# Spreading weight conversion over two rows: fewer steps in batch 0, loads on another queue, block transposes first

## The chip, the cores and the metric

The kernel runs on one core of one Trainium2 chip. The metric is the device time of one execution in microseconds; the kernel before took 1356.45 us (median of three runs, 1355.39 to 1359.32).

## The reference

An attention with a threshold is followed by an MLP mixer. Queries, keys and values are float32; the four MLP weights are float64, because the reference multiplies them by a float64 factor.

```python
# q, k, v: (8, 8, 576, 64) float32
scores = scale * np.matmul(q, k.transpose(0, 1, 3, 2))          # 576 x 576 a head
thresh = np.max(scores, axis=-1, keepdims=True) - tau
scores = np.where(scores >= thresh, scores, -1000000000.0)
attn = np.exp(scores - np.max(scores, axis=-1, keepdims=True))
attn = attn / (np.sum(attn, axis=-1, keepdims=True) + 1e-09)
x = np.matmul(attn, v)            # then (B,H,S,D) -> (B, S, H*D) = (8, 576, 512)
# weights in float64: w_tok1 (576,256), w_tok2 (256,576), w_ch1 (512,1536), w_ch2 (1536,512)
h = np.maximum(x.transpose(0, 2, 1) @ w_tok1, 0.0) @ w_tok2
u = x + h.transpose(0, 2, 1)
out = (u + np.maximum(u @ w_ch1, 0.0) @ w_ch2).astype(np.float32)
```

## The kernel before

The kernel walks through 144 units. A unit is 128 rows of queries for the two heads of a pair; 18 units make a "row", which is one batch (row 0 is batch 0, row 1 is batch 1, and so on). In each unit TensorE makes scores, VectorE takes their maximum, GpSimd turns it into a bias, ScalarE applies Prelu (which does the threshold) and the exponential with its sum, and GpSimd normalizes. Two units later e is transposed, on TensorE in row 0 and by VectorE's 32 x 32 block transposes and sixteen DMAs a group of three units in the other rows. Then come the product with the values and, between the units of the next rows, the MLP of the batch that is done, handed out in small steps by `fill`.

The weights arrive as 64-bit words, in 31 pieces of at most 128 x 512. Each piece is loaded into one of four raw buffers and turned into float32 with integer and float operations on three engines. That is the work which the change moves.

```python
NRAW = 4                                      # raw buffers; one buffer `high` for the upper words
# 31 pieces: 3 of w_tok1, 4 of w_tok2, 12 of w_ch1, 12 of w_ch2

def load_piece(i):
    ...
    nc.sync.dma_start(out=like(raw, dst), in_=src)

def on_scalar(i, part):
        ...
        if part == 0:
            nc.scalar.activation(out=lo.bitcast(I32), in_=lo, func=AF.Copy, scale=2.0**-29)     # L193
        else:
            nc.scalar.activation(out=h2, in_=hi.bitcast(F32), func=AF.Abs)                      # L195

def on_vector(i, part):
        ...
        if part == 0:      # L203: max and mult on h2
        elif part == 1:    # L205: shift left, h2 -> dst
        else:              # L209: sign from hi, or into dst

def on_gpsimd(i):          # L217: dst = dst + lo (int32)

def weight(n):                                # the next n steps; three steps are a piece
    nonlocal steps_done
    for k in range(steps_done, min(steps_done + n, 3 * len(pieces) + 1)):
        i, part = divmod(k, 3)
        if part == 0:
            on_gpsimd(i - 1)
            if i:
                load_piece(i - 1 + NRAW)
        else:
            on_scalar(i + 1, part - 1)
        on_vector(i, part)
        steps_done = k + 1

def weight_to(x):                             # steps up to number x
    weight(max(int(x) - steps_done, 0))

def need(i):                                  # what the MLP calls before it uses piece i
    weight(3 * i + 4 - steps_done)
```

The MLP's channel part, a block of 256 tokens at a time (`ch1` is L507 with its eviction L508, `ch2` is L528):

```python
def ch1(j):
    need(7 + j)
    ...                       # 4 products with wc1[:, j], then ReLU on ScalarE
def ch2(t, part):
    need(7 + NJ + 3 * part + 2)
    if part == 0:
        s["ps"] = ps_mm.tile([P, NCC, P], F32, tag="mm", ...)     # ps_mm has two buffers
    ...                       # 3 products with wc2[:, 3*part ...]
return [(0.0067 * n, lambda j=j: ch1(j)) for j in range(NJ)] + [
    (2.6 if part or b else 3.0, lambda t=t, part=part: ch2(t, part)) for t in range(nt) for part in range(4)
]
```

The loop over units, cut to what orders the instructions (UB is 18, LAG is 2):

```python
for u in range(len(units) + LAG + 4):
    ...
    if on:
        scores(u)                             # L304, L309, L310
    ...
    if 0 < u <= len(units):
        norm(u - 1)                           # L333, L334, L337
    if b_now:
        weight(2)
    else:
        weight_to(2.25 * (u - (1 if visit else 1.5)))
        ...
    if back:
        if not in_blocks(wb):                 # row 0: TensorE transposes, L355, PSUM copies L357
            for i in range(3):
                turn(w, i)
        ...
    if b_now:
        fill(0.4)                             # MLP steps
    if back and in_blocks(wb):
        turn_blocks(w)                        # L367 on VectorE; every third unit 16 DMAs, L376
    if b_now:
        weight(2)
    if on and (b_now or not visit):
        weigh(u)                              # L319 Prelu, L326 exponential, with fill(0.2) three times
    elif b_now:
        fill(0.6)
    if b_now:
        weight(2)
    ...
    else:
        weight_to(2.25 * (u - 1))
    ...                                       # loads of q, k and v, prep (L286), values (L411, L416)
```

Of the kernel before, what the change touches and what calls it, by code (L numbers as in the profile page):

```python
# [9 lines left out]
F32 = mybir.dt.float32  # L10
# [7 lines left out]
P = 128  # L18
# [3 lines left out]
def kernel(  # L22
# [143 lines left out]

    raws = {}

    def load_piece(i):
        if i >= len(pieces):  # L170
            return
        dst, src = pieces[i]
        rows = dst.shape[0]
        n = 1
        for d in dst.shape[1:]:
            n *= d
        raw = raw_at[i % NRAW][0:rows, 0 : n * (2 if wide(i) else 1)].bitcast(src.dtype)
        nc.sync.dma_start(out=like(raw, dst), in_=src)
        if wide(i):
            words = raw.bitcast(U32).rearrange("p (n w) -> p n w", w=2)  # L180
            h2 = high[0:rows, 0:n]
            raws[i] = like(words[:, :, 0], dst), like(words[:, :, 1], dst), like(h2, dst)
        else:
            raws[i] = like(raw, dst)
# [35 lines left out]

    steps_done = 0

    def weight(n):

        nonlocal steps_done
        for k in range(steps_done, min(steps_done + n, 3 * len(pieces) + 1)):
            i, part = divmod(k, 3)
            if part == 0:  # L230
                on_gpsimd(i - 1)
                if i:
                    load_piece(i - 1 + NRAW)
            else:
                on_scalar(i + 1, part - 1)
            on_vector(i, part)
            steps_done = k + 1

    def weight_to(x):

        weight(max(int(x) - steps_done, 0))

    def need(i):

        weight(3 * i + 4 - steps_done)

    load_piece(0)
    load_v(0)
    for i in range(1, NRAW):
# [28 lines left out]
    def in_blocks(b):  # L278
        return b > 0
# [202 lines left out]
    def channel_mlp(b, uT, i):  # L482

        s = {}
        n = min(GR, 2 * S - GR * i)
        nt = n // P

        def turn_u():

            us, ut = s["us"], s["ut"]  # L490
            nc.vector.transpose(
                out=us[:, 0:nt].rearrange("q n a (c d) -> q c (n a) d", c=NCC),
                in_=uT[:, :, GR * i : GR * i + n].rearrange("q c (m r) -> q c m r", r=32),
            )

            def move(a, k):
                nc.sync.dma_start(out=ut[32 * a : 32 * a + 32, 0:nt, k, :], in_=us[32 * k : 32 * k + 32, 0:nt, a, :])

            moves.extend([lambda a=a, k=k: move(a, k) for a in range(4) for k in range(4)])

        def ch1(j):
            need(7 + j)
            if j == 0:
                s["g"] = work.tile([P, NJ, GR], F32, tag="g", bufs=1, name=f"g_{b}_{i}")
            ps = ps_mm.tile([P, GR], F32, tag="mm", name=f"c1_{b}_{i}_{j}")[:, 0:n]
            for c in range(NCC):
                nc.tensor.matmul(ps, lhsT=wc1[:, j, c, :], rhs=uT[:, c, GR * i : GR * i + n], start=(c == 0), stop=(c == NCC - 1))  # L507
            nc.scalar.activation(out=s["g"][:, j, 0:n], in_=ps, func=AF.Relu)  # L508
            if j == 1:
                s["us"] = work.tile([P, GR // P, 4, NCC * 32], F32, tag="us", bufs=1, name=f"us_{b}_{i}")  # L510
                if b:
                    s["ut"] = work.tile([P, GR // P, 4, NCC * 32], F32, tag="ut", bufs=1, name=f"ut_{b}_{i}")
                    turn_u()

        def ch2(t, part):
            need(7 + NJ + 3 * part + 2)
            t0 = GR * i + P * t
            if part == 0:
                s["ps"] = ps_mm.tile([P, NCC, P], F32, tag="mm", name=f"c2_{b}_{i}_{t}")
            ps = s["ps"]  # L520
            flat = ps.rearrange("q c d -> q (c d)")
            if part == 0 and not b:
                for c in range(NCC):
                    nc.tensor.matmul(
                        ps[:, c, :], lhsT=uT[:, c, t0 : t0 + P], rhs=ident, is_transpose=True, start=(c == 0), stop=False, skip_group_check=True
                    )
            for j in range(3 * part, 3 * part + 3):
                nc.tensor.matmul(  # L528
                    flat,
                    lhsT=s["g"][:, j, P * t : P * t + P],  # L530
                    rhs=wc2[:, j, :],
                    start=(j == 0 and b > 0),
                    stop=(j == NJ - 1),
                    skip_group_check=True,
                )
            if part == 3:
                o = s["us"][:, t].rearrange("q a x -> q (a x)")
                if b:
                    move_u()
                    nc.vector.tensor_add(  # L540
                        out=o.rearrange("q (c k d) -> q c k d", c=NCC, k=4),
                        in0=ps.rearrange("q c (k d) -> q c k d", k=4),
                        in1=s["ut"][:, t].rearrange("q k (c d) -> q c k d", c=NCC),
                    )
                else:
                    nc.vector.tensor_copy(out=o, in_=flat)
                nc.sync.dma_start(out=out[b : b + 2].rearrange("b s d -> (b s) d")[t0 : t0 + P, :], in_=o)

        return [(0.0067 * n, lambda j=j: ch1(j)) for j in range(NJ)] + [
            (2.6 if part or b else 3.0, lambda t=t, part=part: ch2(t, part)) for t in range(nt) for part in range(4)  # L550
        ]

    def move_u():
# [42 lines left out]

    prep(0)
    due = deque()
    b_now = 0
    LAG = 2  # L600

    def values_due(u):
# [11 lines left out]
    for u in range(len(units) + LAG + 4):  # L614
        on = u < len(units)
        if u == UB:
            late.close()
            ps_mm = ctx.enter_context(tc.tile_pool(name="ps_mm", bufs=2, space=bass.MemoryType.PSUM))
        if on:
            b_now, p0, t = units[u]  # L620
            n = b_now * NP + p0
        w = u - LAG
        back = 0 <= w < len(units)
        if on:
            scores(u)

        last = False
        visit = False
        if due and not in_blocks(due[0][1]):
            visit = due[0][0] <= u  # L630
            last = values_due(u)
        elif early:
            early.popleft()[1]()
        if 0 < u <= len(units):
            norm(u - 1)
        if b_now:
            weight(2)
        else:


            weight_to(2.25 * (u - (1 if visit else 1.5)))
            if visit and on:
                weigh(u)
        while copies:
            copies.popleft()()
        if last and u < UB:
            early.extend(token_mlp(0, range(NP // 2))[0])
        elif last:
            push(0)
        if back:  # L650
            wb, wp, wt = units[w]
            if not in_blocks(wb):
                for i in range(3):
                    turn(w, i)
            if wt % GU == GU - 1:
                g = wt // GU
                if g < 2:
                    split_middle(wb * NP + wp + g)
                due.append((u + (2 if in_blocks(wb) else 1), wb, wp, g))
        if b_now:  # L660
            fill(0.4)
        if back and in_blocks(wb):
            turn_blocks(w)
        if b_now:
            weight(2)
        if on and (b_now or not visit):
            weigh(u)
        elif b_now:
            fill(0.6)
        if b_now:  # L670
            weight(2)
        elif u == 0:
            on_scalar(0, 0)
            on_scalar(0, 1)
        else:
            weight_to(2.25 * (u - 1))
        if on:


            when = {3: (2, 0, 2), 4: (2, 2, 4), 5: (2, 4, 6), 6: (2, 6, 8), 8: (3, 0, 3), 0: (1, 3, 6), 1: (1, 6, 8)}  # L680
            if u == 0:
                load_qk(1, (nc.sync, nc.sync), range(0, 3))
            if t in when:
                m, lo, hi = when[t]
                if n + m < len(pairs):
                    load_qk(n + m, (nc.scalar if b_now else nc.sync,) * 2, range(lo, hi))
            if t in (3, 7) and n + 2 + t // 4 < len(pairs):
                load_v(n + 2 + t // 4)
            if t == 2:
                prep(n + 1)  # L690
            if t == 7 and n + 2 < len(pairs):
                prep(n + 2)
        if due and in_blocks(due[0][1]):
            values_due(u)

        if back and wt % GU == 0 or not on:
            move_u()
# [31 lines left out]
```

## Time and profile before

| what | us |
|---|---|
| time, median of three | 1356.45 |
| span of the profiled run | 1354.5 |
| TensorE matmul busy | 1308.3 |
| VectorE busy | 591.7 |
| ScalarE busy | 585.5 |
| GpSimd busy | 355.2 |
| conversion on VectorE (L203, L205, L209, all 31 pieces) | 63.0 |
| last conversion step begins (L217) | 188.3 |

The profile names engines PE (TensorE), DVE (VectorE), ACT (ScalarE), POOL (GpSimd) and SP (SyncE); a q behind the name is the engine's queue, where DMAs are issued. L numbers are lines of the kernel. A line of the timeline has the start, the length, the engine and line, what is written from what, and in brackets the idle time before it and who ended it. The row of conversion on VectorE is the sum of that engine's groups for those three lines (18.0, 19.0 + 3.8 and 17.5 + 4.7 us).

### The profile page before, as it was taken

To read this page: it belongs to the slowest core of one execution; us is meant where nothing else is said; L and a number is where in the kernel's file an instruction comes from. 1 tells how busy PE (TensorE), PEld (TensorE's weight loads), DVE (VectorE), ACT (ScalarE), POOL (GpSimd) and SP (SyncE) were. 2 spreads that over 40 slices of the span, in tenths; PEclk is the share of its full clock that TensorE was granted. 3 is DMA by queue.
4 is the path that set the end of the run, shared out by engine and by line. 5 is a ranking of instruction groups with operands and counts; after the bars stand their busy time and mean duration, and the time that the engine had idled before them with its cause. 6 is when DMAs were issued, how large, how long until landed. Compare 5 with 4: busy or idle time off the path is not lost.

```text
span 1354.5 us, 17794 instructions
## 1 busy us (share of the span) xinstructions
PE 1308.3 (97%) x6138; PEld 810.6 (60%) x6138; DVE 591.7 (44%) x1024; ACT 585.5 (43%) x1299; POOL 355.2 (26%) x683
## 2 busy tenths in 40 slices
PE   6888899999999999999999999999999999999998
PEld 4555656547574666565665567565656566575675
DVE  6878874435443444434344444435443454201000
ACT  6776654444444444443434444344333454120110
POOL 4565652222322222212122222222121222100000
PEclk9998999999999999999999999999999999999999
DMA  5434764545354444443445435534443453400000
GB/s 122 116 90 119 203 167 100 122 95 128 90 131 95 105 106 106 120 109 86 93 101 126 103 79 128 126 81 112 112 101 83 114 117 77 114 21 17 23 24 32
DMA packets 296539, 135.31 MB, mean 100 GB/s; under 512 B 204737, under 2 KB 289217, under 8 KB 296449
## 3 DMA queue, kind: packets, MB, share of 16 engines
q1 hardware_dynamic: 167840, 118.15, 34.2%
q10 hardware_dynamic: 128608, 16.01, 7.4%
q8 instruction: 49, 0.80, 0.3%
q14 instruction: 42, 0.34, 0.1%
HBM read 43.25 MB, written 9.44 MB: 39 GB/s over the span
## 4 chain that ended last, share of the span: by engine, by line
PE 87%; DVE 5%; ACT 3%; DMA 2%; SPq 1%; issue 1%; POOL 1%; ACTq 0%; DVEq 0%; POOLq 0%
PE c L507 27%; PE c L528 27%; PE sc L304 11%; PE pv L416 9%; PE t L454 5%; PE t L464 4%; PE pv L411 3%; DVE mx L309 2%; ACT e L319 1%; PE tx L447 1%; SPq L376 1%; PE tr L355 1%; DMA lk<-in_k_dram 1%; ACT e L326 1%; DVE wc L205 0%
## 5 line engine op out<-in xcount | busy, mean ns | idle before, releaser
L309 DVE TENSOR_REDUCE mx<-sc 128x1 f32<-128x576 f32 x288 | 204.2, 749 | 449.1 <-PE sc L304 448.9
L507 PE MATMUL c<-xT,wc 128*128 128x256 f32 (+1 forms) x1920 | 400.0, 362 | 0.1
L528 PE MATMUL c<-wc,g 128*128 128x512 f32 x864 | 389.5, 597 | 0.0
L507 PEld LDWEIGHTS c<-xT,wc 128*128 128x128 f32 x1920 | 334.3, 190 | 69.8 <-issue 29.7
L310 POOL TENSOR_SCALAR bias<-mx,toff 128x1 f32<-128x1 f32 x288 | 82.9, 288 | 777.1 <-DVE mx L309 721.2
L319 ACT ACTIVATE e<-sc,bias 128x576 f32<-128x576 f32 x288 | 199.5, 740 | 178.7 <-POOL bias L310 178.0
L528 PEld LDWEIGHTS c<-wc,g 128*128 128x128 f32 x864 | 158.9, 190 | 181.6 <-issue 178.1
L326 ACT ACTIVATE e<-e,ntau 128x576 f32<-128x576 f32 x288 | 221.1, 772 | 0.0
L337 POOL TENSOR_SCALAR e<-e,rr 128x576 f32<-128x576 f32 x288 | 215.2, 760 | 14.0 <-ACT g L508 2.6
L508 ACT ACTIVATE g<-c 128x256 f32<-128x256 f32 (+1 forms) x240 | 87.0, 362 | 295.9 <-PE c L507 285.8
L304 PE MATMUL sc<-kT,qT 64*128 64x288 f32 (+1 forms) x1280 | 194.9, 437 | 11.8 <-DVE kT L286 7.4
L367 DVE STREAM_TRANSPOSE T<-e 128x1152 f32<-128x1152 f32 x126 | 171.9, 1365 | 5.5 <-DMA eT<-T 3.1
L304 PEld LDWEIGHTS sc<-kT,qT 64*128 64x128 f32 (+1 forms) x1280 | 108.0, 180 | 98.8 <-issue 57.2
L416 PE MATMUL pv<-eT,lv 128*64 128x384 f32 (+1 forms) x1024 | 138.2, 411 | 0.0
L416 PEld LDWEIGHTS pv<-eT,lv 128*64 128x64 f32 x1024 | 77.0, 139 | 50.1 <-issue 41.3
L421 ACT COPY xT<-pv 128x384 f32<-128x384 f32 (+1 forms) x56 | 21.0, 400 | 167.6 <-PE pv L416 164.4
L540 DVE TENSOR_TENSOR us<-c,ut 128x512 f32<-128x512 f32 x27 | 18.6, 690 | 155.0 <-PE c L528 140.3
L464 PE MATMUL t<-w,a 128*128 128x288 f32 x256 | 75.2, 421 | 8.0 <-DVE xT L468 4.7
L454 PE MATMUL t<-x_sb,w 128*128 128x512 f32 (+1 forms) x180 | 73.2, 554 | 0.0
L464 PEld LDWEIGHTS t<-w,a 128*128 128x128 f32 x256 | 45.8, 192 | 30.1 <-issue 10.5
L468 DVE TENSOR_TENSOR xT<-xT,t 128x288 f32<-128x288 f32 x64 | 28.3, 446 | 71.0 <-PE t L464 70.5
L326 ACT ACTIVATION_READ_ACCUMULATOR e<-e,ntau 128x1 f32 x288 | 56.7, 197 | 0.0
(46 smaller groups left out, 542.3 us busy)
## 6 DMA issues: line engine op xcount, KB each, us to landing
eT<-T SPq DMA_DIRECT2D x672, 108.0 KB, 2.3
scratch<-in_moe_w_ch_dram SPq DMA_DIRECT2D x24, 512.0 KB, 3.6
lv<-in_v_dram SPq DMA_DIRECT2D x32, 288.0 KB, 3.3
out_dram<-us SPq DMA_DIRECT2D x36, 256.0 KB, 2.2
lk<-in_k_dram ACTq DMA_DIRECT2D x111, 72.0 KB, 2.8
lq<-in_q_dram ACTq DMA_DIRECT2D x106, 72.0 KB, 2.3
ut<-us SPq DMA_DIRECT2D x192, 32.0 KB, 1.9
lq<-in_q_dram SPq DMA_DIRECT2D x22, 72.0 KB, 3.4
```

Of the source, the lines that this page charges most:

```text
L304: nc.tensor.matmul(sc[h][rows, f, 0:HS], lhsT=qT[r, cols], rhs=kT[r, HS * f : HS * f + HS], start=True, stop=True)
L309: nc.vector.tensor_reduce(out=mx[:, c], in_=sc[h][:, :, 0:HS], axis=AX.XY, op=ALU.max)
L319: nc.scalar.activation(out=eh, in_=sc[h][:, :, 0:HS], func=AF.Prelu, bias=bias[:, h : h + 1], scale=SCALE, alpha=STEEP)
L326: nc.scalar.activation(out=eh, in_=eh, func=AF.Exp, bias=ntau, accum_out=rs[:, h : h + 1])
L337: nc.gpsimd.tensor_scalar(out=eh, in0=eh, scalar1=rr[:, h : h + 1], scalar2=1.0, op0=ALU.mult, op1=ALU.mult)
L367: nc.vector.transpose(out=T[:, :, place, :].rearrange("p a (c x) -> p c a x", c=NK), in_=e.rearrange("p (c a x) -> p c a x", c=NK, a=4))
L416: nc.tensor.matmul(to[r], lhsT=lv[:, j, :], rhs=e[j], start=False, stop=(c == NI - 1), skip_group_check=True)
L454: nc.tensor.matmul(to, lhsT=w1[:, t, P * m : P * m + P], rhs=x_sb[:, t, cols], start=(t == 0), stop=(t == NT - 1))
L464: nc.tensor.matmul(to, lhsT=a[:, m, P * c : P * c + P], rhs=w2[:, m, HS * f : HS * f + HS], start=(m == 0), stop=(m == NTK - 1))
L507: nc.tensor.matmul(ps, lhsT=wc1[:, j, c, :], rhs=uT[:, c, GR * i : GR * i + n], start=(c == 0), stop=(c == NCC - 1))
L508: nc.scalar.activation(out=s["g"][:, j, 0:n], in_=ps, func=AF.Relu)
L528: nc.tensor.matmul(flat, lhsT=s["g"][:, j, P * t : P * t + P], rhs=wc2[:, j, :], start=(j == 0 and b > 0), stop=(j == NJ - 1), skip_group_ ...
```

## The change

The conversion has 94 steps. Before, row 0 does 36 of them at 2.25 a unit, and row 1 does two steps at three places of each unit. After, row 0 stops at 24 steps at 1.75 a unit, and row 1 does 6.2 steps a unit at two places: behind `fill(0.4)`, and behind `weigh`. In row 1 raw loads are issued from ScalarE's queue, once a unit behind `weigh`, so that they no longer stand behind the block moves of e on SyncE's queue. In row 1 the block transpose of e comes directly behind maxima and reciprocals, ahead of the MLP's steps and of conversion. The first block's `ch2` steps go by part, with both token tiles in turn, so that the last pieces of w_ch2 are asked for later. The aim is to relieve VectorE and ScalarE in row 0, where TensorE has little else to do, and to put the work where TensorE is full.

```diff
-    def load_piece(i):
+    asked = 0
+    def load_piece(i, eng=nc.sync):
+        nonlocal asked
+        asked = i + 1
         ...
-        nc.sync.dma_start(out=like(raw, dst), in_=src)
+        eng.dma_start(out=like(raw, dst), in_=src)
         ...
     def weight(n):
             ...
-                if i:
+                if i and not b_now:
                     load_piece(i - 1 + NRAW)
             else:
+                if asked == i + 1 < len(pieces):
+                    load_piece(asked, nc.scalar)
                 on_scalar(i + 1, part - 1)
             ...
+    def reload():
+        while asked < min((steps_done - 1) // 3 + NRAW, len(pieces)):
+            load_piece(asked, nc.scalar)
         ...
     def channel_mlp(b, uT, i):
         ...
-                s["ps"] = ps_mm.tile(...)
-            ps = s["ps"]
+                s[t] = ps_mm.tile(...)
+            ps = s[t]
         ...
+        last = [(t, part) for t in range(nt) for part in range(4)]
+        if b == 0 and i == 0:
+            last.sort(key=lambda x: x[1])
         ...
+    WROW = 24
+    WRATE = 6.2
         ...
-        if b_now:
-            weight(2)
-        else:
-            weight_to(2.25 * (u - (1 if visit else 1.5)))
+        if not b_now:
+            weight_to(min(1.75 * (u - (1 if visit else 1.5)), WROW))
         ...
             if not in_blocks(wb):
                 for i in range(3):
                     turn(w, i)
+            elif b_now == 1:
+                turn_blocks(w)
         ...
         if b_now:
             fill(0.4)
-        if back and in_blocks(wb):
+            weight_to(WROW + WRATE * (u - UB + 0.3))
+        if back and in_blocks(wb) and b_now != 1:
             turn_blocks(w)
-        if b_now:
-            weight(2)
         if on and (b_now or not visit):
             weigh(u)
         elif b_now:
             fill(0.6)
         if b_now:
-            weight(2)
+            reload()
+            weight_to(WROW + WRATE * (u - UB + 0.9))
         ...
         else:
-            weight_to(2.25 * (u - 1))
+            weight_to(min(1.75 * (u - 1), WROW))
```

More of the change, by code (lines that the diff above doesn't have):

```diff
@@ L245, in need @@
         weight(3 * i + 4 - steps_done)
+    b_now = 0
     load_piece(0)
@@ L518, in ch2 @@
             if part == 0:
-                s["ps"] = ps_mm.tile([P, NCC, P], F32, tag="mm", name=f"c2_{b}_{i}_{t}")
-            ps = s["ps"]
+                s[t] = ps_mm.tile([P, NCC, P], F32, tag="mm", name=f"c2_{b}_{i}_{t}")
+            ps = s[t]
             flat = ps.rearrange("q c d -> q (c d)")
@@ L547, in ch2 @@
                 nc.sync.dma_start(out=out[b : b + 2].rearrange("b s d -> (b s) d")[t0 : t0 + P, :], in_=o)
+        last = [(t, part) for t in range(nt) for part in range(4)]
+        if b == 0 and i == 0:
+            last.sort(key=lambda x: x[1])
         return [(0.0067 * n, lambda j=j: ch1(j)) for j in range(NJ)] + [
-            (2.6 if part or b else 3.0, lambda t=t, part=part: ch2(t, part)) for t in range(nt) for part in range(4)
+            (2.6 if part or b else 3.0, lambda t=t, part=part: ch2(t, part)) for t, part in last
         ]
@@ L598 @@
     due = deque()
-    b_now = 0
+    WROW = 24
+    WRATE = 6.2
     LAG = 2
```

## The prediction

> **What bounds the kernel now.** I read the share of busy time first, then the slices, then busy time by stretches, then the chain of waits and the timeline of the two places where the slices show a loss. Shares and slices of the page:
>
> ```profile
> PE 1308.3 (97%) x6138; PEld 810.6 (60%) x6138; DVE 591.7 (44%) x1024; ACT 585.5 (43%) x1299; POOL 355.2 (26%) x683
> ...
> PE   6888899999999999999999999999999999999998
> DVE  6878874435443444434344444435443454201000
> PEclk9998999999999999999999999999999999999999
> ```
>
> TensorE (PE) is the bound of the whole, but not of the first five slices of 33.9 us: there it is at 6 to 8 tenths and VectorE (DVE) is at 7 to 8. Busy time by stretches puts numbers to that (columns: stretch, length, busy time of PE, weight load, DVE, ACT, POOL, granted clock, DMA share, GB/s):
>
> ```profile
> 10.00:99.00 89.00, 74.31 (x458) 46.86 (x456) 71.67 (x153) 70.76 (x151) 54.13 (x89) 1.00 0.44 99
> 99.00:165.00 66.00, 56.64 (x259) 37.16 (x259) 55.19 (x93) 42.91 (x89) 37.55 (x46) 0.90 0.59 163
> 165.00:240.00 75.00, 74.45 (x349) 46.23 (x349) 46.73 (x77) 41.62 (x92) 33.59 (x56) 1.00 0.56 133
> ```
>
> TensorE idles 89.0 - 74.3 = 14.7 us in row 0 (batch 0, up to the scores of unit 18 at 98.9 us), 66.0 - 56.6 = 9.4 us in the next 66 us, and 0.6 us in the 75 after that. So whatever the change can win lies before 165 us: 24 us of idle time and some slow clock (0.90 in the second stretch). After 165 us TensorE loses 14.2 us in 1189, and the change leaves nearly all of that code alone.
>
> The second stretch has two places worth showing. The first, from the timeline (start, length, engine, line; in brackets the idle time before and who ended it):
>
> ```profile
> 111.28 0.41 DVE L203 TENSOR_SCALAR scratch<-scratch 128x512 f32<-128x512 f32 x1
> 111.72 0.86 DVE L205 TENSOR_SCALAR wc<-scratch 128x512 uint32<-128x512 uint32 x1
> 112.51 0.54 DVE L357 COPY eT<-tr 128x384 f32<-128x384 f32 x1
> 113.10 0.90 PE L355 MATMUL tr<-ident,e 128*128 128x128 f32 x3 [2.63 <-DVE eT L357]
> ```
>
> Two conversion steps stand on VectorE ahead of the PSUM copy that TensorE's next transposes wait for. After this 2.63 us gap the clock falls: the eight score matmuls that follow took 2.9 us in all, against 1.24 us elsewhere. The second place, from the timeline, two queues and two engines:
>
> ```profile
> 143.17 10.63 SPq L376 DMA_DIRECT2D eT<-T  x16
> 153.91 9.46 SPq L178 DMA_DIRECT2D scratch<-in_moe_w_ch_dram  x5
> 157.48 0.69 ACT L193 ACTIVATE scratch<-scratch 128x512 int32<-128x512 uint32 x1 [4.66 <-DMA scratch<-in_moe_w_ch_dram]
> 161.42 1.86 PE L304 MATMUL sc<-kT,qT 64*128 64x288 f32 x8 [1.61 <-ACT e L319]
> ```
>
> The loads of raw weights stand on SyncE's queue behind sixteen issues of block moves (10.6 us). ScalarE waits 4.7 us for a load, its Prelu for the next unit (L319) comes late, and TensorE waits 1.6 us for the score slot.
>
> **What the Trainium skill says.** "DMA: Bandwidth & Descriptors", section Issuing engines are not separate DMA queues, says that transfers issued by different engines run on the same sixteen DMA engines, so that a second issuer saves only the sequencer's time to issue. Here that time is what counts: 10.63 us for sixteen issues. The trace agrees. "SBUF — State Buffer", section SBUF: two separate sides, says that VectorE and GpSimd share a port pair which one instruction holds to its end, so that the other blocks. The trace fits: the same L203 takes 0.41 us at its median and up to 1.51 us, L205 0.44 and up to 1.46 us. So a conversion step costs more in a crowded stretch. "TensorE: Matmul & The Clock Gate", section What's actually happening, says that an idle window of about 3.4 us halves the clock. The trace shows the slower clock near the two longest gaps: 0.66 in 110 to 120 us, 0.83 in 140 to 150 us.
>
> **The change part by part.** A piece of weights costs three steps: VectorE L203, L205, L209 (means 582, 791, 729 ns, together 2.10 us), two ScalarE activations (639 and 643 ns, 1.28 us) and one GpSimd add (1.43 us).
>
> 1. Twelve steps fewer in row 0 are four pieces: 4 x 2.10 = 8.4 us of VectorE, 5.1 us of ScalarE, 5.7 us of GpSimd that leave row 0. Not all was on the path. In the chain of waits from 8 to 99 us the pieces of conversion (L193, L195, L203, L205, L209, L217) add up to 10.0 us for the 36 steps, 0.28 us a step; twelve steps are 12 x 0.28 = 3.3 us. Taken: -3.5 us, with 8.4 us the most it could be if VectorE were the only bound.
> 2. The twelve steps come back in row 1. In the order of VectorE's instructions, units 18 to 21 hold 24 conversion steps in both kernels; the remaining 46 (34 before) fall on units 22 to 29 instead of 22 to 27. There TensorE is full (74.45 of 75 us) and VectorE has 28 us free in those 75. The 8.4 us fit. Taken: 0.
> 3. In units 18 and 19 conversion now stands behind the PSUM copies (it moved behind the MLP's steps). That takes 0.41 + 0.86 = 1.3 us from the 2.63 us gap and part of the slow clock after it (about 1.7 us too long in the scores, 1.5 us in the values product: 5.06 against 3.6 us). Taken: -2 us, as the five steps behind the copies delay the next maximum instead.
> 4. Loads on ScalarE's queue end the 10.6 us hold-up: ScalarE's waits for loads sum to 12.9 us between 99 and 240 us. TensorE felt 1.6 us at 161 us, and about 0.6 us in each of some four later units whose scores took 1.8 to 1.9 instead of 1.24 us. At most 4 us.
> 5. Against that, the block transpose of e (1.36 us) moves ahead of all conversion in row 1. ScalarE's absolute value (L195) waits for the L205 of the piece before, since they share one buffer, and Prelu stands behind it in ScalarE's order. So Prelu can come up to 1.4 us later in units 22 to 28, where fewer steps (2 to 3, not 4) stand ahead of it. I set 4 and 5 together at -1.5 us.
> 6. The second matmuls of the MLP's first block alternate between its two token tiles, so that the last pieces of weights are needed later. TensorE's other instructions keep their order, and its work is the same. 0 by itself; it only keeps part 2 from stalling.
>
> Sum: -3.5 - 2 - 1.5 = -7 us; from 1356.45 that is 1349.5. I shade it to 1349, since a stall avoided also avoids slow clock.
>
> **Rivals.** (a) Conversion comes late in row 1: the first MLP then demands its pieces and TensorE waits for wc. For it: twelve steps fewer in hand at unit 18. Against: the first L507 needs step 25, and the order has 48 done by unit 22; the demand of L507 (three steps each, three a unit) overtakes 6.2 a unit only for three or four units, which start 20 steps ahead. It would give about 1357 to 1362. (b) Prelu behind the transpose and behind load issues (0.35 to 0.5 us each on ScalarE) holds the scores by about 1 us in eight units: the win of row 0 is halved, 1352 to 1355. (c) Row 0 is bound by the loop from scores through maximum, Prelu, exponential and transposes, so that fewer conversion steps only give VectorE idle time: row 0 wins 1 us, total 1353. For it: VectorE 81% and ScalarE 80% busy, neither full. (d) Row 0 takes all 8.4 us and the clock stays up through 99 to 165 us: 1338 to 1341.
>
> **Range and chances.** Steps 1 and 3 could be nothing or double, 4 and 5 could be +3 or -4. From (b), (c) to (d) I take 1340 to 1357. 2% is 27 us; all idle time before 165 us is 24 us plus the start, so faster by over 2% needs nearly all of it: 0.03. Slower by over 2% would need a new stall in rows that are not touched: 0.02. Within: 0.95.
>
> **What would show it.** The scores of unit 18 begin near 95 us instead of 98.9 (step 1). The gap before the transposes of unit 19 (2.63 us) is under 1.5 us and the clock of 99 to 165 us is above 0.93 (step 3). ScalarE's waits for raw loads fall from 12.9 us to under 4, and the last L217 ends about 10 us later than 188 us (steps 2 and 4). Score matmuls in units 22 to 29 stay at or under 1.9 us (5). I am wrong if L507 or L528 wait for wc, or if row 0 is no shorter.

## The result: 1.2% slower, and where the time went

The changed kernel took 1370.81 us (median, 1370.03 to 1374.81), the kernel before 1355.39 us beside it: a ratio of 1.0117, 95% interval 1.0096 to 1.0138. Predicted were 1349 us, with 1340 to 1357 as the range.

Shares and slices of the page after:

```profile
PE 1307.2 (96%) x6138; PEld 809.4 (59%) x6138; DVE 592.5 (43%) x1024; ACT 585.5 (43%) x1299; POOL 344.4 (25%) x683
...
PE   6887779999999999999999999999999999999998
DVE  5778766345444454434433445424433454201000
PEclk9999899999999999999999999999999999999999
```

No engine works noticeably more than before (VectorE most, 592.5 us against 591.7); TensorE's row now has sevens in slices 4 to 6. The same stretches as before the change (stretch, length, busy time of PE, weight load, DVE, ACT, POOL, granted clock, DMA share, GB/s):

```profile
10.00:99.00 89.00, 76.64 (x476) 49.14 (x473) 65.31 (x144) 67.17 (x145) 46.21 (x86) 1.00 0.41 87
99.00:165.00 66.00, 49.73 (x232) 31.61 (x230) 51.38 (x88) 38.96 (x78) 32.73 (x44) 0.92 0.46 127
165.00:240.00 75.00, 65.42 (x283) 39.52 (x283) 50.55 (x80) 40.91 (x87) 32.36 (x51) 0.93 0.62 157
```

TensorE gains 2.3 us of busy time in row 0. It loses 56.6 - 49.7 = 6.9 us in the second stretch and 74.5 - 65.4 = 9.0 us in the third. A table of when the first maximum of a unit begins shows it step by step:

| unit | before, us | after, us | difference |
|---|---|---|---|
| 0 | 9.7 | 11.1 | +1.4 |
| 18 | 101.1 | 97.9 | -3.2 |
| 22 | 137.8 | 137.0 | -0.8 |
| 23 | 146.3 | 149.4 | +3.1 |
| 26 | 172.2 | 176.8 | +4.6 |
| 27 | 180.0 | 190.1 | +10.1 |
| 29 | 192.6 | 212.0 | +19.4 |
| 36 | 242.3 | 259.2 | +16.9 |
| 37 | 255.9 | 269.7 | +13.8 |

Row 0 is 4.6 us shorter (the run starts 1.4 us later and is 3.2 us ahead at unit 18). Then units 22 to 29 lose over 20 us: those that hold the rest of the conversion. From unit 37 on the distance stays between 13.4 and 14.2 us.

What ScalarE waits for between 99 and 240 us, after (us in total, times, longest):

```profile
ACT scratch L197 <- DMA scratch<-in_moe_w_ch_dram: 21.8, 14, 3.2
ACT scratch L199 <- DVE wc L209: 13.5, 7, 3.0
```

Before, the same two (there named L193 and L195, waiting for L205) were:

```profile
ACT scratch L193 <- DMA scratch<-in_moe_w_ch_dram: 12.9, 6, 5.5
...
ACT scratch L195 <- DVE wc L205: 5.4, 7, 1.3
```

The worst place, timeline after (start, length, engine, line; in brackets the idle time before and its releaser):

```profile
195.73 0.84 ACTq L182 DMA_DIRECT2D scratch<-in_moe_w_ch_dram  x2
...
199.35 0.67 ACT L197 ACTIVATE scratch<-scratch 128x512 int32<-128x512 uint32 x1 [2.14 <-DMA scratch<-in_moe_w_ch_dram]
...
204.56 0.67 ACT L199 ACTIVATE scratch<-scratch 128x512 f32<-128x512 f32 x1 [2.64 <-DVE wc L209]
205.14 1.35 ACT L332 ACTIVATE e<-sc,bias 128x576 f32<-128x576 f32 x2
205.92 2.91 PE L317 MATMUL sc<-kT,qT 64*128 64x288 f32 x8 [6.17 <-ACT e L332]
```

Two loads are asked for at 195.73, on ScalarE's queue, and ScalarE's next conversion step needs one of them. It stands until 199.35. The chain of waits after runs through this stretch so (start, length, what):

```profile
195.73 3.59 DMA scratch<-in_moe_w_ch_dram
...
200.24 0.32 ACT scratch L199
...
200.59 0.43 DVE scratch L207
201.01 1.33 DVE mx L322 x2
...
202.53 1.36 DVE T L380
203.89 0.65 DVE wc L209
...
205.14 0.73 ACT e L332
...
205.92 2.91 PE sc L317 x7
```

This is a loop of one unit, from 195.7 to 206: the load, ScalarE's absolute value, VectorE's L207, the maximum behind it, the block transpose, L209, ScalarE's next absolute value (it shares its buffer with the L209), Prelu, and the scores of the next unit. Each piece of this chain starts when the one before it ends. TensorE feels it as waits for Prelu between 99 and 240 us, first before, then after:

```profile
PE sc L304 <- ACT e L319: 3.3, 3, 1.6
...
PE sc L317 <- ACT e L332: 11.6, 6, 6.2
```

### The profile page after: what moved, and what is told of

Read it like the earlier page. It is cut to its first block, busy times and chain, and to the rows that moved or that the text cites. A ratio compares the mean times of both kernels' runs of the same rounds, so it can differ in the third digit from the quotient of the medians.

```text
span 1368.2 us, 17772 instructions
## 1 busy us (share of the span) xinstructions
PE 1307.2 (96%) x6138; PEld 809.4 (59%) x6138; DVE 592.5 (43%) x1024; ACT 585.5 (43%) x1299; POOL 344.4 (25%) x683
## 4 chain that ended last, share of the span: by engine, by line
PE 84%; DVE 5%; ACT 4%; DMA 4%; issue 1%; POOL 1%; SPq 1%; ACTq 0%; DVEq 0%; POOLq 0%
PE c L541 26%; PE c L520 26%; PE sc L317 11%; PE pv L429 8%; PE t L467 5%; PE t L477 4%; PE pv L424 3%; DVE mx L322 2%; ACT e L332 2%; DMA scratch<-in_moe_w_ch_dram 1%; DMA lk<-in_k_dram 1%; PE tr L368 1%; PE tx L460 1%; ACT e L339 1%; DVE T L380 1%
## 5 line engine op out<-in xcount | busy, mean ns | idle before, releaser
L520 PE MATMUL c<-xT,wc 128*128 128x256 f32 (+1 forms) x1920 | 403.2, 364 | 2.8 <-ACT g L521 2.7
L541 PE MATMUL c<-wc,g 128*128 128x512 f32 x864 | 390.5, 598 | 0.0
L520 PEld LDWEIGHTS c<-xT,wc 128*128 128x128 f32 x1920 | 336.1, 191 | 73.5 <-issue 30.1
L323 POOL TENSOR_SCALAR bias<-mx,toff 128x1 f32<-128x1 f32 x288 | 79.0, 275 | 789.4 <-DVE mx L322 731.8
L541 PEld LDWEIGHTS c<-wc,g 128*128 128x128 f32 x864 | 159.4, 190 | 182.5 <-issue 179.3
L350 POOL TENSOR_SCALAR e<-e,rr 128x576 f32<-128x576 f32 x288 | 211.4, 746 | 15.5 <-ACT g L521 2.6
```

The lines of the kernel that those rows point to most:

```text
L350: nc.gpsimd.tensor_scalar(out=eh, in0=eh, scalar1=rr[:, h : h + 1], scalar2=1.0, op0=ALU.mult, op1=ALU.mult)
L541: nc.tensor.matmul(flat, lhsT=s["g"][:, j, P * t : P * t + P], rhs=wc2[:, j, :], start=(j == 0 and b > 0), stop=(j == NJ - 1), skip_group_ ...
```

## The experiments

Every run was compared with the kernel before on the same chip. First the list, then each run. "Asks" means where raw loads are issued in row 1; "transpose" and "burst" mean the places of e's block transpose and of the unit's first conversion steps. Where two runs are compared below, the difference of their ratios has a 95% margin, worked out from the two intervals as if they were independent; 0.0010 is 1.4 us.

| run | what it is | ratio | 95% interval |
|---|---|---|---|
| changed kernel | all parts | 1.0117 | 1.0096 to 1.0138 |
| e1_ask_twice | changed, two asks a unit | 1.0067 | 1.0049 to 1.0086 |
| e2_ask_on_sync | changed, loads as before | 1.0129 | 1.0112 to 1.0146 |
| e3_blocks_late | changed, transpose late | 1.0091 | 1.0069 to 1.0113 |
| e4_row0_only | before, 24 steps in row 0 | 1.0078 | 1.0058 to 1.0098 |
| e5_row0_and_parts | e4 with alternating parts | 1.0001 | 0.9993 to 1.0010 |
| e6_twice_and_late | changed, both mends | 1.0019 | 1.0010 to 1.0029 |
| e7_blocks_early_only | before, transpose early | 1.0003 | 0.9991 to 1.0016 |
| e8_row0_full | changed, 36 steps in row 0 | 1.0084 | 1.0062 to 1.0107 |
| e9_early_and_behind | before, transpose early, burst behind MLP | 1.0158 | 1.0140 to 1.0176 |
| e10_sync_and_late | changed, loads as before, transpose late | 1.0049 | 1.0031 to 1.0068 |
| e11_thirty_and_parts | before, 30 steps, alternating parts | 1.0011 | 0.9999 to 1.0023 |
| e12_twice_in_before | e5, two asks a unit on ScalarE | 1.0036 | 1.0025 to 1.0046 |
| e13_first_burst_ahead | changed, burst ahead of MLP | 1.0144 | 1.0124 to 1.0164 |
| e14_behind_only | before, burst behind MLP | 1.0071 | 1.0046 to 1.0096 |
| e15_ahead_and_twice | e13 with two asks | 1.0048 | 1.0029 to 1.0067 |
| e16_late_ask_only | before, one late ask on ScalarE | 1.0030 | 1.0019 to 1.0041 |
| e17_gpsimd_loads_24 | e5, loads from GpSimd | 1.0065 | 1.0050 to 1.0081 |
| e18_gpsimd_loads_36 | before, loads from GpSimd | 1.0076 | 1.0050 to 1.0102 |

### Loads: when they are asked for

**e1_ask_twice.**

```diff
         if b_now:
+            reload()
             fill(0.4)
             weight_to(WROW + WRATE * (u - UB + 0.3))
```

> The changed kernel with raw loads asked for at two places of each unit of row 1 instead of one: also ahead of the first MLP steps, when the buffers freed by the last burst of conversion are known. Loads stay on ScalarE's queue. T1 (loads are asked for directly ahead of the steps that need them, so ScalarE stands 14 times, 21.8 us, for data): most of the loss in units 22 to 29 goes, 1353 to 1359, and ScalarE's waits for raw loads fall under 6 us. R1 (the block transposes ahead of conversion hold Prelu): no gain, 1367 to 1371. R2 (too many conversion steps are left for row 1): no gain, 1367 to 1371. R3 (ScalarE's time to issue loads): no gain, as many issues as before.

1363.55 us, 1.0067: T1's direction, but outside its range. The second ask takes 0.0050 ± 0.0028, some 7 us of the 16. ScalarE's waits after the mend:

```profile
ACT scratch L199 <- DVE wc L209: 17.3, 10, 3.7
...
ACT scratch L197 <- DMA scratch<-in_moe_w_ch_dram: 3.2, 3, 2.1
```

The waits for loads are nearly gone (21.8 to 3.2 us), the waits behind the transpose are not (13.5 to 17.3 us). The same number of issues on ScalarE remains, so R3 does not explain what came back.

**e2_ask_on_sync.**

```diff
-                if i and not b_now:
+                if i:
                     load_piece(i - 1 + NRAW)
...
-            reload()
```

> The changed kernel with the loads alone undone: asked for as soon as a buffer is free, on SyncE's queue, as in the kernel before; everything else as changed. T1: 1353 to 1360, the hold-ups behind the block moves come back (some 5 to 13 us of ScalarE's waits) but not the 14 of them. R1: 1366 to 1371. R2: 1366 to 1371. R3: 1353 to 1360, so it tells R3 from T1 only together with the run that asks twice.

1370.94 us, 1.0129: no gain, against T1's number (0.0012 ± 0.0027 above the changed kernel). The timeline of this run shows a hold-up:

```profile
144.94 6.63 SPq L387 DMA_DIRECT2D eT<-T  x7
...
151.69 2.83 SPq L182 DMA_DIRECT2D scratch<-in_moe_w_ch_dram  x4
155.21 0.65 ACT L197 ACTIVATE scratch<-scratch 128x512 int32<-128x512 uint32 x1 [7.43 <-DMA scratch<-in_moe_w_ch_dram]
...
156.54 2.92 PE L315 MATMUL sc<-kT,qT 64*128 64x288 f32 x8 [6.29 <-ACT e L330]
```

With transposes early, their moves come before the loads in SyncE's order, and a load is 7.4 us late. ScalarE waited 14.5 us for loads in all, in two waits. Back on SyncE the loads only change one hold-up for another.

**e16_late_ask_only.**

```diff
+    # load_piece, weight and reload as in the changed kernel
         if b_now:
+            reload()
             weight(2)          # the last pair of the unit
```

> The kernel before with one part of the change alone: in row 1 the raw loads are asked for once a unit, behind the exponentials, on ScalarE's queue. Conversion (three pairs a unit, 36 steps in row 0) and transposes as before. Theory Q: the loads come just ahead of their use, ScalarE waits 15 to 22 us for them, ratio 1.004 to 1.008. Theory P: with the burst ahead of the MLP there is slack, ratio 0.999 to 1.003.

1360.61 us, 1.0030 (1.0019 to 1.0041): at P's upper edge, below Q's range. By itself the late ask costs 4 us. ScalarE's waits ahead of its first conversion step:

```profile
ACT scratch L197 <- DMA scratch<-in_moe_w_ch_dram: 6.5, 5, 2.3
ACT scratch L197 <- DMA eT<-T: 4.4, 1, 4.4
...
ACT scratch L197 <- POOL wc L221: 3.9, 4, 1.1
```

Only 6.5 us are waits for a load itself, not 15 to 22. But the 3.9 us belong to the ask as well: the issue on ScalarE's queue waits for GpSimd's add, which frees the buffer. In the wait of 4.4 us the load had landed; ahead of the step stood the issue of a key load, which waited for a block move. The profiled execution is the longest of fourteen (1365.14 us) and was 4.6 us behind at unit 18, ahead of anything that the edit changes.

**e13_first_burst_ahead.**

```diff
-        if not b_now:
+        if b_now:
+            weight_to(WROW + WRATE * (u - UB + 0.3))
+        else:
...
             fill(0.4)
-            weight_to(WROW + WRATE * (u - UB + 0.3))
```

> The changed kernel with one part undone: in row 1 the unit's first burst of conversion stands directly behind the reciprocals, ahead of the block transpose and of the MLP's first steps. Loads are asked for once a unit as changed. Theory P (the place of that burst decides, because Prelu stands behind the burst's last absolute value on ScalarE, and that behind the transpose on VectorE): ratio 1.003 to 1.007, ScalarE's waits for VectorE's shift step under 7 us instead of 13.5. Theory Q (late asking is the larger part): 1.007 to 1.010, with the waits for loads still near 20 us.

1375.62 us, 1.0144: no faster than the changed kernel (0.0027 ± 0.0029 above it), a miss for both theories. ScalarE's waits for the shift step fell as P said, but those for loads rose:

```profile
ACT scratch L197 <- DMA scratch<-in_moe_w_ch_dram: 28.5, 15, 4.0
...
ACT scratch L199 <- DVE wc L209: 4.7, 6, 1.4
```

The unit's second burst and the next unit's first now follow each other directly behind the one ask, so all 6.2 steps of a unit come just after it. That this is the reason is read from the order of the program; the next run bears it out.

**e15_ahead_and_twice.**

```diff
+            reload()
             weight_to(WROW + WRATE * (u - UB + 0.3))     # ahead of the MLP, as in e13
```

> The changed kernel with two mends: the first burst ahead of the block transpose and the MLP's steps, and loads asked for at two places of a unit, ScalarE's queue. Block transposes early as changed. If place and late asking make up the loss: ratio 0.997 to 1.001. If raw loads on ScalarE's queue that run at the same time as the sixteen block moves slow these (5.9 us of wait for values in the run with loads asked twice in the kernel before), 1.002 to 1.005.

1363.15 us, 1.0048, in the second range. One line more took 0.0096 ± 0.0028, 13 us, from e13. ScalarE still waited 13.4 us for loads.

### The transpose ahead of conversion

**e3_blocks_late.**

```diff
-            elif b_now == 1:
-                turn_blocks(w)
...
-        if back and in_blocks(wb) and b_now != 1:
+        if back and in_blocks(wb):
             turn_blocks(w)                 # behind fill(0.4) and the first burst
```

> The changed kernel with the block transposes of e in row 1 put back behind the MLP's first steps and the conversion that follows them; loads as changed. T1: little, 1365 to 1370, because ScalarE still stands for loads; at most the 1.4 us of one transpose for each of some five units. R1: the loss goes, 1352 to 1358. R2: no gain.

1365.46 us, 1.0091: T1's range at its lower end, not R1's. The gain over the changed kernel, 0.0026 ± 0.0030, is not clear of the spread. ScalarE's waits for L209 fell from 13.5 to 3.9 us, those for loads rose from 21.8 to 29.5 us.

**e6_twice_and_late**: the edits of e1 and e3 together.

> The changed kernel with both mends: asking for loads at two places of a unit, and block transposes late. Theory A: the two gains (7.3 and 5.3 us) are of one loop a unit (load, ScalarE's two activations, VectorE's L207, maximum, transpose, L209, absolute value, Prelu, scores), so together they give at least their sum, 1351 to 1359. Theory B: at most the better of the two, 1362 to 1366.

1358.10 us, 1.0019: theory A. In pairs of runs the second ask is worth 0.0050 ± 0.0028 (changed to e1) and 0.0072 ± 0.0024 (e3 to e6), the late transpose 0.0026 ± 0.0030 (changed to e3) and 0.0048 ± 0.0021 (e1 to e6). Together they take 0.0098 ± 0.0023 of the 0.0117. That each is worth more where the other is already mended lies within the margins and is not shown.

**e10_sync_and_late**: the edits of e2 and e3 together.

> The changed kernel with both the loads (SyncE, as soon as a buffer is free) and the block transposes (late) of before; fewer steps in row 0, two bursts a unit and the alternating parts as changed. Putting back the loads alone gave nothing (1.0129). A1 and A2: that was because the early transposes put their sixteen issues on SyncE ahead of the loads; with the transposes late the loads come in time again: ratio 1.000 to 1.004, waits of ScalarE for loads of 10 to 15 us. If it stays over 1.008, the two bursts a unit are a cost of their own that was not seen.

1362.13 us, 1.0049, just over the range. With the loads on SyncE in both, the late transpose takes 0.0080 ± 0.0025 from e2; ScalarE's waits for loads were 12.8 us, inside what was expected. So e2's failure came with the early transposes. What e10 has beyond e5 (1.0001, below) is only the two bursts of conversion a unit and their places, so these cost 0.0048 ± 0.0020 here, 6.5 us.

**e7_blocks_early_only.**

```diff
+            elif b_now == 1:
+                turn_blocks(w)
...
-        if back and in_blocks(wb):
+        if back and in_blocks(wb) and b_now != 1:
```

> The kernel before with one part of the change alone: in row 1 the block transpose of e stands directly behind the maxima and reciprocals. 36 steps in row 0, loads and conversion as before. Theory A (Prelu waits for the absolute value L195, that for L205, and L205 now for 1.36 us of transpose in each of some nine units): 1358 to 1364. Theory B: 1352 to 1357, as the number of steps left is that of before.

1356.91 us, 1.0003: theory A's number was wrong, the early transpose by itself costs nothing that can be measured. Two conversion steps still stood ahead of it.

**e9_early_and_behind**: e7, and the first pair of steps moved as well.

```diff
-        if b_now:
-            weight(2)              # directly behind norm
...
             fill(0.4)
+            weight(2)
```

> The kernel before with the two moves in row 1 together: block transpose directly behind the maxima, and the unit's first two conversion steps behind the MLP's first steps (so all conversion stands behind the transpose). 36 steps in row 0, loads on SyncE as before. Theory A1 (the transpose costs where every conversion step of the unit stands behind it, because the absolute value that Prelu waits for then comes 1.4 us later; with two steps ahead of it, it cost nothing): 1359 to 1364, ratio 1.003 to 1.006, and ScalarE's waits for VectorE's shift step rise from 6 us to over 10. A2 (it costs only in company of loads that are asked for late): ratio 0.999 to 1.002.

1378.16 us, 1.0158: A1's direction, and more than twice the upper end of its range. TensorE's waits for Prelu between 99 and 240 us are the largest of all runs:

```profile
PE sc L304 <- ACT e L319: 22.1, 7, 5.8
```

**e14_behind_only**: the move of the pair without the early transpose.

> The kernel before with one move: in row 1 the unit's first two conversion steps stand behind the MLP's first steps; block transposes late as before, directly behind these two steps and ahead of the next two. Theory P1 (the place behind the MLP's steps costs by itself): ratio over 1.006. Theory P2 (it costs only where the transpose, 1.36 us, stands ahead of the first burst): 0.999 to 1.003.

1365.22 us, 1.0071: P1. Conversion behind the MLP's steps costs 10 us by itself, the early transpose on top of it another 12 (e9). ScalarE's waits for L205 were 14.1 us here, 5.4 before: all four steps ahead of Prelu now stand behind the MLP's steps. Two places show what this does to TensorE:

```profile
107.92 0.67 ACT L195 ACTIVATE scratch<-scratch 128x512 f32<-128x512 f32 x1 [1.40 <-DVE wc L205]
109.27 2.92 PE L304 MATMUL sc<-kT,qT 64*128 64x288 f32 x8 [2.97 <-ACT e L319]
...
119.97 2.91 PE L304 MATMUL sc<-kT,qT 64*128 64x288 f32 x8 [3.73 <-ACT e L319]
```

TensorE's waits for the PSUM copy ahead of the transposes fell from 3.0 to 0.3 us, as step 3 of the prediction wanted, but the shift step and with it the absolute value and Prelu come later. From unit 18 to 21 the run falls from 1.4 to 8.2 us behind.

### The steps of row 0

**e4_row0_only.**

```diff
-            weight_to(2.25 * (u - (1 if visit else 1.5)))
+            weight_to(min(1.75 * (u - (1 if visit else 1.5)), 24))
...
-            weight_to(2.25 * (u - 1))
+            weight_to(min(1.75 * (u - 1), 24))
```

> The kernel before with only the numbers of row 0 changed: 1.75 steps a unit up to 24; row 1 as before (three times two steps a unit, loads on SyncE's queue as soon as a buffer is free, block transposes late). T1: the 4.6 us that row 0 won stay, less what row 1 pays for two more units of conversion: 1350 to 1356. R2 (36 steps in row 0 were needed so that row 1 keeps pace): 1364 to 1372.

1364.69 us, 1.0078: R2's range. The run is some 2.5 us ahead up to unit 25 and 10.5 us behind at unit 30. Between them the timeline has:

```profile
202.43 3.78 PE L528 MATMUL c<-wc,g 128*128 128x512 f32 x4 [5.02 <-POOL wc L217]
```

The last pieces of w_ch2 are demanded before they are converted.

**e5_row0_and_parts**: e4, with the alternating parts of `ch2` as in the change.

> The kernel before with two parts of the change: 24 steps in row 0, and the second matmuls of the first MLP block alternating between its two token tiles. Loads (SyncE, as soon as a buffer is free), block transposes (late) and conversion (three times two steps a unit) as before. Theory A (three separate costs: late asking, transposes ahead of conversion, and, where nothing else is changed, the last pieces of w_ch2 asked for too early): the 6 us of waits of L528 for the add L217 go, and row 0 keeps its win of about 3 us: 1350 to 1355. Theory B (only the number of steps left for row 1 counts): as the run with the numbers of row 0 alone, 1362 to 1366.

1355.12 us, 1.0001 (0.9993 to 1.0010): the waits of L528 are gone and with them the loss of e4. But the win is gone too: 4.2 us ahead at unit 27, level at unit 28, where the chain of waits has one raw load of 6.46 us ahead of an L193, an L195 and a late Prelu.

**e11_thirty_and_parts**: as e5, with 2.0 steps a unit up to 30.

> The kernel before with 30 steps in row 0 (2.0 a unit) and the alternating parts. If what 24 steps win in row 0 (3 to 4 us) is lost again because the last two pieces come in units 28 and 29, 30 steps keep half of the win and lose less: ratio 0.997 to 0.999. If the loss sits in one hold-up of a load (6.5 us at 178 us), it may come at any number: 0.999 to 1.001.

1.0011 (0.9999 to 1.0023): no gain at 30 either.

**e8_row0_full**: the changed kernel with 2.25 steps a unit up to 36 and WROW at 36.

> The changed kernel with the numbers of row 0 alone undone: 2.25 steps a unit up to 36; loads asked once a unit on ScalarE's queue, transposes early, 6.2 steps a unit from 36 on. Theory A: the loop of a unit is as long but runs for two units fewer, row 0 loses its 3 us: 1363 to 1371. Theory B: 1353 to 1358.

1367.17 us, 1.0084: theory A. The number of steps is not what made the change slow: with 36 steps most of the loss stays (0.0033 ± 0.0031 less).

### Can the win of row 0 be kept?

**e12_twice_in_before**: e5, with `reload()` ahead of the first and of the last pair of a unit, on ScalarE's queue.

> The kernel before with 24 steps in row 0, the alternating parts, and raw loads on ScalarE's queue in row 1 asked for at two places of a unit, each ahead of a pair of conversion steps; transposes late, three pairs a unit. The run with the first two parts alone ended even with before (1.0001): it was 4 us ahead up to unit 27 and lost them to a load that stood behind the block moves. Theory A: with the loads off SyncE that hold-up goes and the win of row 0 stays: ratio 0.996 to 0.999, ScalarE's waits for loads under 6 us. Rival (24 steps leave too much for row 1, whatever the loads): 1.000 to 1.003.

1360.96 us, 1.0036: just over the rival's range, and for a reason that neither named. Up to unit 24 it is 6.2 us ahead, at unit 25 only 0.5. Between them TensorE stands ahead of the values product, whose operand is moved by the sixteen DMAs of the block transpose:

```profile
156.90 1.54 PE L423 MATMUL pv<-eT,vl 128*64 128x384 f32 x4 [5.89 <-DMA lk<-in_k_dram]
```

The product reads no key load; the view names the transfer that landed last at that moment. The last of the block moves landed at 156.60.

**e17_gpsimd_loads_24** and **e18_gpsimd_loads_36**: e5 and the kernel before, each with

```diff
-        nc.sync.dma_start(out=like(raw, dst), in_=src)
+        (nc.gpsimd if b_now else nc.sync).dma_start(out=like(raw, dst), in_=src)
```

> The kernel before with 24 steps in row 0, the alternating parts, and in row 1 each raw load issued from GpSimd's queue directly behind the add that frees its buffer. If the win of row 0 was lost only to loads that stood in line or were asked for late: ratio 0.996 to 0.999, ScalarE's waits for loads under 5 us. If GpSimd's work to issue (it also makes the bias that Prelu waits for, and normalizes e) or the transfers beside the block moves cost as much: 1.000 to 1.005.

> The kernel before with one difference: in row 1 each raw load is issued from GpSimd's queue directly behind the add that frees its buffer. If the hold-up of loads behind the block moves (12.9 us of ScalarE's waits) cost TensorE what the prediction gave it: ratio 0.997 to 0.999. If TensorE had other work at the time: 0.999 to 1.002.

1363.53 us, 1.0065, and 1363.79 us, 1.0076: both above all that was expected. ScalarE's waits for loads fell only to 8.1 and 7.6 us. TensorE waits at the same place as in e12; this is e18:

```profile
164.84 1.55 PE L412 MATMUL pv<-eT,vl 128*64 128x384 f32 x4 [6.36 <-DMA eT<-T]
```

No version of this study beats the kernel before.

## Why the prediction was wrong

Measured against the prediction's own steps, the loss divides so:

| steps | forecast, us | measured | from |
|---|---|---|---|
| 1, 2 and 6: fewer steps in row 0, alternating parts | -3.5 | 0.0001 ± 0.0009, 0 us | e5 |
| 3: conversion in two bursts, behind the MLP's steps | -2 | 0.0048 ± 0.0020, 6.5 us | e10 over e5 |
| 4 and 5: loads on ScalarE, transposes early | -1.5 | 0.0068 ± 0.0028, 9.2 us | changed kernel over e10 |

This is one order of putting the parts in; in another the shares differ. Between 4 and 5 the order decides: from e10, early transposes cost 0.0080 ± 0.0025 (e2) and the loads on top of them -0.0012 ± 0.0027; taken first, the loads cost 0.0042 ± 0.0029 (e3) and the transposes on top 0.0026 ± 0.0030. So the steps that failed are 3 and, taken together, 4 and 5.

**Step 1 was right.** Twelve steps fewer in row 0 were to give 3.5 us. The changed kernel gained 4.6 us up to unit 18, and all twelve kernels with 24 steps began unit 18 ahead of the kernel before, by 1.6 to 5.1 us. Single traces spread: six other kernels with 36 steps lay between 1.3 us ahead and 4.6 behind. VectorE's busy time from 10 to 99 us fell from 71.7 to 65.3 us.

**Step 2 failed in part.** "The 8.4 us fit. Taken: 0." They fit as busy time, and still the win did not survive row 1, even with loads and order of before (e5, e11). From unit 18 to the end e5 loses 3.3 us to the kernel before, and the changed kernel 16.6 us where e8, with 36 steps done in row 0, loses 11.5: 3 to 5 us for the twelve steps, in single traces. Free time of an engine was counted where a chain of waits runs across engines. The last conversion begins at 216.5 us, 28 us later than before and not 10.

**Step 3 was wrong.** The gap ahead of the transposes of unit 19 did not shrink, it is 2.92 us (2.63 before), because the maximum, with the steps of unit 18 ahead of it, stands before the copies in any case:

```profile
108.64 0.90 PE L368 MATMUL tr<-ident,e 128*128 128x128 f32 x3 [2.92 <-DVE eT L370]
```

The granted clock from 99 to 165 us is 0.92, under the 0.93 that was to be passed. And the move of conversion behind the MLP's steps, which was to gain 2 us, cost 6.5 us in e10 and 10 us in e14: where the gap at the transposes did close, Prelu came late instead.

**Step 4 failed as well, and in its mechanism.** "Loads on ScalarE's queue end the 10.6 us hold-up." I read only which queue a load stands in, not when it is asked for relative to the step that needs it. The change asks once a unit, directly ahead of a burst, on the engine that then needs the data. ScalarE's waits were to fall from 12.9 to under 4 us and rose to 21.8 us, 14 waits instead of 6. One ask a unit instead of two costs 0.0050 to 0.0096, by what else is changed. Against loads on SyncE the single ask gains nothing that is clear of the spread (e2 to the changed kernel, e10 to e3, e16), while two asks gain 0.0062 ± 0.0025 (e2 to e1) and 0.0030 ± 0.0021 (e10 to e6). So in the changed kernel's order of steps the time of the ask was wrong and not the queue. In the order of before, two asks on ScalarE's queue cost 0.0035 ± 0.0014 (e5 to e12).

**Step 5 had the mechanism and the wrong size and sign.** Prelu does come late behind transpose and L209; I gave 4 and 5 together -1.5 us. The late transpose is worth 0.0026 ± 0.0030 to 0.0080 ± 0.0025 (4 to 11 us), by where the loads are. The place of conversion behind the MLP makes it dear: alone the early transpose costs 0.0003 (e7), on top of that place 0.0087 ± 0.0031 (e14 to e9). In the changed kernel that place can't be taken back alone, since the one ask a unit then starves it (e13).

**Step 6 was right**: the alternating parts are what keeps 24 steps from costing 10 us (e4 against e5).

**The rivals.** (a) did not happen: neither L520 nor L541 ever waits for wc in the changed kernel. (b) was right in kind, with "about 1 us in eight units"; single waits for Prelu reached 6.2 us. (c) is refuted by row 0, and (d) by row 1. One reading of the prediction is off without harm: TensorE idles 14.7 us after 165 us, not 14.2.

What stays open: the 0.0019 of e6 is not divided further. It has the same bursts as e10 (1.0049), so what these cost depends on the loads too. And the parts do not add: alone they are 0.0001 (row 0 and parts), 0.0003 (transpose), 0.0030 (ask), 0.0071 (burst behind), sum 0.0105, which is near 0.0117 only by chance, as e9 alone is over its own two parts by 0.0084.

## What to carry to other kernels

Ahead of moving work to where an engine has free time, write down the loop that a unit of that stretch runs through across the engines, with every engine it passes twice; what is put on that loop can cost time however much of the engine is free. For a load count the steps between its issue and its use, not only which queue it stands in: asked for just ahead of its use, on the queue of the engine that needs it, it leaves that engine standing for what is left of the landing (21.8 us in 14 waits here). A move of several parts should be tried part by part and in pairs, since here a part that is free alone and one that costs 10 us alone cost 21 us together (e9).

## What the runs showed of the hardware that was not expected

Taking the raw loads off SyncE's queue slowed the block moves that stayed on it, in the kernels with late block transposes. Issues and their median time to landing in us between 140 and 175 us, first the kernel before (all on SyncE):

```profile
eT<-T SPq DMA_DIRECT2D x24, 108.0 KB, 3.3
```

and e18, where the loads come from GpSimd:

```profile
scratch<-in_moe_w_ch_dram POOLq DMA_DIRECT2D x6, 512.0 KB, 4.9
eT<-T SPq DMA_DIRECT2D x16, 108.0 KB, 5.6
```

In e12 and e16, with loads on ScalarE's queue, the moves took 5.2 and 5.3 us, in e17 4.3. In e12 two moves issued at 146.42 and 147.05 landed after 2.2 us, and the five from 147.69 to 150.31, with two raw loads issued at 147.70 and 148.15, after 4.5 to 6.5 us. With early transposes the median stays low: 2.3 us in the changed kernel, 2.2 in e1, 2.3 in e15, all with loads on ScalarE's queue. So slow landing is not what made the changed kernel slow.

A second thing happens beside it. In the changed kernel the sixteen issues of a group of moves still stand in one stretch, and it is longer than the 10.63 us of before:

```profile
139.97 14.94 SPq L389 DMA_DIRECT2D eT<-T  x16
```

By the trace SyncE stood from 147.16 to 151.72 us inside it, until a raw load that ScalarE had issued at 146.59 was in. So another queue for the loads did not keep them out of the moves' way. In e12 such a stop, from 143.63 to 146.40, lasted until an earlier move had landed.

So the line on SyncE, which the prediction took for a pure cost, also kept the 512 KB loads behind the moves from running beside them, and TensorE waits for these moves next. That the transfers share the same engines is what the Trainium skill states, in "DMA: Bandwidth & Descriptors" under Issuing engines are not separate DMA queues; that the second issuer saves "only" issue time is not all that happened here. That contention on the DMA engines is the cause in e12, e17 and e18 is inferred from the landing times; it was not tested by taking the loads away, and no run separates it from the issues that stood.
